# Duo attention and a one-slot-per-token expert layer on one core: loads, constants and steps put in another order

## The chip, the cores and the metric

The kernel runs on one core of a Trainium2 chip. Its engines are TensorE (PE, with its weight loads as PEld), VectorE (DVE), ScalarE (ACT), GpSimd (POOL) and SyncE (SP); sixteen DMA engines move data for the core. The metric is the device time of one execution in microseconds (us). TensorE's clock has two levels, 1.2 and 2.4 GHz, and the profile gives the granted clock as a share of the upper one.

## The reference

Attention first: 4 batches, 8 heads, 768 positions, 64 channels a head. Heads 0, 2 and 6 see all earlier positions; the other five see the first 4 positions and the last 64. The result, as a matrix of 3072 tokens by 512 columns, then goes through a layer of 8 experts in which a token uses at most one.

```python
scores = scale * np.matmul(q, k.transpose(0, 1, 3, 2))
stream_keep = causal & (is_sink | in_win)        # 4 sinks, window of 64
mask = np.where(retr[0, :, 0, 0, None, None], full_mask, stream_mask)
a = softmax(np.where(mask, scores, -1e9))
x = np.matmul(a, v)                               # -> [3072, 512]
...
do_compute = x @ w_skip > 0                       # the others keep x
e_idx = np.argmax(xc @ w_gate, axis=1)
gate_w = probs[np.arange(len(xc)), e_idx]
for e in range(8):                                # w1[e]: 512x1024, w2[e]: 1024x512
    h = np.maximum(xc[mask] @ w1[e], 0.0)
    y[mask] = gate_w[mask, None] * (h @ w2[e])
out[do_compute] = xc + y
```

## The kernel before

The program is written out by hand: instructions stand on each engine in the order in which the Python code makes them, and the framework adds the waits that data and buffers need. There is no scheduler, so a step that stands late in an engine's row, or that waits there, holds up all that stands behind it on that engine.

**Attention.** The loop at L554 goes over the four batches, b0 to b3. Each has six slots (`slots`, L524), and a slot is a few steps: `T(pr)` transposes q and k of a pair of heads (`trans`, L272: PE, then ACT copies qT and DVE copies kT), `R` makes the scores and exponentials of a full head (`retr`, L300: PE, then ACT), `X` those of a windowed head (`strm`, L322), `sinks` those of the four sink positions. The step `"o"` is `outs(g)` (L514): for row block g of the batch before, it multiplies the exponentials with v (`outp`, L359), normalises on DVE, stores the block to the output from SP's queue, and makes transposes (`xt`) and gate logits (`gates`) of earlier blocks. So v of a batch is used in the slots of the next one; `prep_v(b)` (L265), four DVE copies that shift v by half a block, is the first to wait for v of batch b.

**Loads.** All loads are issued from POOL's queue and cast fp32 to fp16 on the way: q and k of a batch (`load_qk`), v of a batch (`load_v`), the weights of an expert (`load_w`). There are two buffers for q and k, two for v, four for the weights of experts 0 to 3; the weights of experts 4 and 5 go into the buffers of q and k, those of 6 and 7 into memory that attention has left. `after_t` (L541), called in the slots, and the lines L572 to L575 between the batches issue them.

**Routing.** `route(c0, n)` (L412) makes, from the gate logits of n of the 24 row blocks, each token's expert and its place in a table; it is a generator, and `go_on` (L510) runs its next part. The first call takes blocks 0 to 11 in batch b3; after the last blocks of attention (the loop at L577, the tail) the second takes blocks 12 to 23.

**Experts.** With the table known, POOL gathers the rows of each expert, 2 tiles of 128 rows each (`gather`), and issues the last weights in between. Per expert PE makes the transposes (`xin`), the first product (`up_`) and the second (`down`), and POOL scatters the two tiles back to the output. The first scatter waits for every gather, since both touch the output tensor.

`fills` and the loops over `fp` are matmuls that no one reads.

## Time and profile before

| | |
|---|---|
| median of 3 runs | 260.56 us (260.16 to 263.18) |
| the profiled execution's own time | 263.12 us |
| its span in the profile | 261.3 us |
| PE busy | 189.6 us, 73% of the span |
| DVE busy | 115.3 us, 44% |
| ACT busy | 89.4 us, 34% |
| bytes read from memory | 56.66 MB |

No engine is busy throughout, and the share of an engine over the whole span mixes stages: the time is read stage by stage, by what ends the idle time in each. A busy time of POOL at a load is its issue; the data land later, which shows in the waits for them and in the rate of the DMA engines. The profiled execution took 2.56 us more than the median.

### The profile page before, as it was taken

To read this page: it belongs to the slowest core of one execution; us is meant where nothing else is said; L and a number is where in the kernel's file an instruction comes from. 1 tells how busy PE (TensorE), PEld (TensorE's weight loads), DVE (VectorE), ACT (ScalarE), POOL (GpSimd) and SP (SyncE) were. 2 spreads that over 40 slices of the span, in tenths; PEclk is the share of its full clock that TensorE was granted. 3 is DMA by queue.
4 is the path that set the end of the run, shared out by engine and by line. 5 is a ranking of instruction groups with operands and counts; after the bars stand their busy time and mean duration, and the time that the engine had idled before them with its cause. 6 is when DMAs were issued, how large, how long until landed. Compare 5 with 4: busy or idle time off the path is not lost.

```text
span 261.3 us, 5338 instructions
## 1 busy us (share of the span) xinstructions
PE 189.6 (73%) x2288; PEld 123.2 (47%) x2288; DVE 115.3 (44%) x280; ACT 89.4 (34%) x125; POOL 72.8 (28%) x84
## 2 busy tenths in 40 slices
PE   6302697769988706975939667997669999959960
PEld 2201354456765405654626344452456677726620
DVE  0008168467774025676693322471054454415430
ACT  3100575666683401582333432100232322313100
POOL 8605850031332000311000000006883400762260
PEclk9855599999995665897577955699799999999996
DMA  5999999999999999999970221103799993240110
GB/s 77 173 159 191 68 176 206 205 230 239 238 232 236 198 186 224 227 235 194 225 169 16 108 83 40 43 0 88 205 195 233 208 225 138 85 177 4 48 58 12
DMA packets 53138, 39.55 MB, mean 151 GB/s; under 512 B 27945, under 2 KB 44329, under 8 KB 53104
## 3 DMA queue, kind: packets, MB, share of 16 engines
q0 software_dynamic: 49648, 32.82, 84.7%
q1 hardware_dynamic: 3456, 6.29, 7.0%
q8 instruction: 20, 0.33, 0.5%
q14 instruction: 14, 0.11, 0.1%
HBM read 56.66 MB, written 10.49 MB: 257 GB/s over the span
## 4 chain that ended last, share of the span: by engine, by line
PE 53%; DMA 16%; DVE 12%; ACT 8%; issue 5%; POOL 3%; POOLq 0%; DVEq 0%; ACTq 0%
DMA va<-in_v_dram 15%; PE mhp L662 11%; PE myp L679 11%; PE sps L263 6%; ACT atr L319 5%; DVE x L384 3%; PE sps L315 3%; PE tps L277 3%; PE tps L398 3%; PE sps L329 2%; PE sps L311 2%; PE av L371 2%; ACT x L390 1%; PE mtp L646 1%; DMA xg<-out_dram,idg 1%
## 5 line engine op out<-in xcount | busy, mean ns | idle before, releaser
L319 ACT ACTIVATE atr<-sps 128x1024 f16<-128x1024 f32 (+1 forms) x36 | 31.5, 915 | 38.7 <-PE sps L315 38.7
L617 POOL DMA_INDIRECT xg<-out_dram,idg x16 | 16.5, 1029 | 68.4 <-DVE gs L608 59.2
L263 PE MATMUL sps<-esk,ident 128*128 128x512 f16 x90 | 27.7, 448 | 4.9 <-ACT atr L319 2.7
L398 PE MATMUL tps<-ident,x 128*128 128x128 f16 x96 | 11.5, 256 | 20.7 <-DVE x L392 10.9
L662 PE MATMUL mhp<-mxT,w1t 128*128 128x256 f16 x192 | 22.8, 278 | 4.0 <-issue 3.3
L683 POOL DMA_INDIRECT out_dram<-xg,idx x16 | 16.3, 1018 | 31.4 <-issue 17.3
L346 ACT ACTIVATE ats<-sps 128x768 f16<-128x768 f32 x20 | 15.4, 810 | 26.7 <-PE sps L340 26.7
L311 PE MATMUL sps<-tri,idl 64*128 64x128 f16 x144 | 12.4, 238 | 14.8 <-DVE tri L147 10.4
L662 PEld LDWEIGHTS <-w1t 128*128 128x128 f16 x192 | 19.3, 100 | 8.2 <-issue 5.0
L679 PE MATMUL myp<-w2t,ht 128*128 128x512 f16 x96 | 22.2, 379 | 0.0
L108 POOL DMA_DIRECT2D va<-in_v_dram x8 | 11.4, 1438 | 38.5 <-PE av L379 38.5
L283 DVE COPY kT<-tps 128x768 f16<-128x768 f16 x16 | 15.1, 947 | 15.5 <-PE tps L277 15.5
L681 DVE SCALAR_TENSOR_TENSOR xg<-myp,gs,xg 128x512 f32<-128x512 f32 x16 | 12.0, 751 | 22.1 <-PE myp L679 14.8
L398 PEld LDWEIGHTS <-x 128*128 128x128 f16 x96 | 6.8, 111 | 28.0 <-DVE x L392 11.4
L666 DVE TENSOR_SCALAR ht<-mhp 128x512 f16<-128x512 f32 x16 | 11.1, 691 | 17.1 <-PE mhp L662 15.0
L315 PE MATMUL sps<-qT,kT 64*128 64x512 f16 (+3 forms) x96 | 16.4, 352 | 3.0 <-DVE kT L283 3.0
L679 PEld LDWEIGHTS <-ht 128*128 128x128 f16 x128 | 12.3, 98 | 12.2
L668 ACT ACTIVATE ht<-mhp 128x512 f16<-128x512 f32 x16 | 9.6, 598 | 24.2 <-issue 12.9
L311 PEld LDWEIGHTS <-idl 64*128 64x128 f16 x144 | 8.0, 102 | 18.1 <-DVE idl L146 10.4
L283 ACT COPY qT<-tps 128x768 f16<-128x768 f16 x16 | 12.8, 800 | 10.3 <-PE tps L277 10.1
L263 PEld LDWEIGHTS <-ident 128*128 128x128 f16 x90 | 8.6, 107 | 15.5 <-issue 8.9
L651 ACT COPY mxT<-mtp 128x512 f16<-128x512 f16 x15 | 8.2, 588 | 19.2 <-PE mtp L646 13.1
(156 smaller groups left out, 342.7 us busy)
## 6 DMA issues: line engine op xcount, KB each, us to landing
w1t<-in_moe_w_dram POOLq DMA_DIRECT2D x6, 1024.0 KB
w2t<-in_moe_w_dram POOLq DMA_DIRECT2D x6, 1024.0 KB
out_dram<-x SPq DMA_DIRECT2D x24, 256.0 KB, 5.7
va<-in_v_dram POOLq DMA_DIRECT2D x8, 384.0 KB
qin<-in_q_dram POOLq DMA_DIRECT2D x3, 768.0 KB
kin<-in_k_dram POOLq DMA_DIRECT2D x3, 768.0 KB
qin<-in_moe_w_dram POOLq DMA_DIRECT2D x2, 1024.0 KB
kin<-in_moe_w_dram POOLq DMA_DIRECT2D x2, 1024.0 KB
```

Of the source, the lines that this page charges most:

```text
L263: nc.tensor.matmul(ps[:, :512], ident, fill, start=True, stop=True)
L283: eng(t.rearrange("c (p n) -> c p n", n=NT), ps.rearrange("c n p -> c p n"))
L311: nc.tensor.matmul(ps[i][:, x:x + P], idl[rows[i], u], tri[rows[i], u], start=(u == 0), stop=False, skip_group_check=True)
L315: nc.tensor.matmul(ps[i][:, x:x + n], kT[b, pr][rows[i], j * P:(j + 1) * P], qT[b, pr][rows[i], q0:q0 + n], start=False, stop=True, skip_g ...
L319: nc.scalar.activation(at[b, PAIRS[pr][i]][:, o:o + w], ps[i][:, :w], ACT.Exp, scale=SCALE)
L346: nc.scalar.activation(a, ps[i][:, :S], ACT.Exp, scale=SCALE)
L398: nc.tensor.matmul(ps[:, s], xs[g][:, s * P:(s + 1) * P], ident, is_transpose=True, start=(s == 0), stop=(s == DS - 1))
L617: nc.gpsimd.indirect_dma_start(out=xg[e, t], out_offset=None, in_=out[:, :], in_offset=bass.IndirectOffsetOnAxis(ap=idg[:, sl:sl + 1], axi ...
L662: nc.tensor.matmul(hp[:, u], w1t[:, s, f * P:(f + 1) * P], xT[:, s], start=(s == 0 and u == 0), stop=(s == DS - 1 and u == 1))
L679: nc.tensor.matmul(yp, hts[e][:, f, t * P:(t + 1) * P], w2t[:, f], start=(f == 0), stop=(f == FS - 1))
L681: nc.vector.scalar_tensor_tensor(xg[e, t], yp, gs[:, sl:sl + 1], xg[e, t], ALU.mult, ALU.add)
L683: sc = nc.gpsimd.indirect_dma_start(out=out[:, :], out_offset=bass.IndirectOffsetOnAxis(ap=idx[:, sl:sl + 1], axis=0), in_=xg[e, t], in_of ...
```

## The change

Seven edits stand in the diff. (1) The memsets of the ones column of both v buffers stand ahead of the first loads, and `vsk`'s memset stands in `consts_1`. (2) `load_qk(1)` goes ahead of `load_v(0)`. (3) Weights: `load_w(0)` moves from `consts_2` to `after_t(0)`, experts 1 to 4 to a new function `after_o` at the end of a batch, behind the load of v, and expert 5 into the expert stage, behind the first four gathers. (4) The slots hold their steps in another order, `prep_v` one slot later, `sinks` one slot earlier, and `go_on` is called once in a slot instead of twice. (5) Routing is done in three calls of 12, 6 and 6 blocks. (6) In the tail, `outp` of a block stands ahead of `xt` and `gates` of earlier ones; in the expert stage `cast(1)` stands ahead of `up_(0)`, and `xin(1)` in its middle. (7) Pools: the buffers of exponentials and v are in two pools by parity of the batch, qT has three buffers instead of four, and the expert tiles are taken from attention's space with waits tile by tile.

```diff
--- before.py
+++ after.py
@@ -81,13 +81,17 @@
     qkp = ctx.enter_context(tc.tile_pool(name="qkp", bufs=2))
     att = ExitStack()
-    ac = att.enter_context(tc.tile_pool(name="ac", bufs=1))
+    qtp = att.enter_context(tc.tile_pool(name="qtp", bufs=3))
+    par = [att.enter_context(tc.tile_pool(name=f"par{i}", bufs=1)) for i in range(2)]
+    xp = att.enter_context(tc.tile_pool(name="xp", bufs=3))
     q_in, k_in = {}, {}
-    va = [ac.tile([P, H, NT, V1], FP16, name=f"va{i}") for i in range(2)]
-    vs = [ac.tile([P, 5, NT, V1], FP16, name=f"vs{i}") for i in range(2)]
+    va = [par[i].tile([P, H, NT, V1], FP16, name=f"va{i}") for i in range(2)]
+    vs = [par[i].tile([P, 5, NT, V1], FP16, name=f"vs{i}") for i in range(2)]
     wts = {}
     def load_qk(b, split=False):
@@ -117,9 +121,11 @@
     rel_i = const.tile([P, P], I32, name="rel_i")
     nc.gpsimd.iota(rel_i, pattern=[[1, P]], base=0, channel_multiplier=-1)
+    for i in range(2):
+        nc.vector.memset(va[i][:, :, :, D:], 1.0)
     load_qk(0, True)
+    load_qk(1)
     load_v(0)
-    load_qk(1)
     esk = [const.tile([P, S], FP16, name=f"esk{i}") for i in range(2)]
@@ -131,8 +137,6 @@
     nc.vector.memset(ones, 1.0)
     warm = const.tile([P, 1], FP32, name="warm")
     nc.scalar.activation(warm, ones[:, :1], ACT.Exp)
-    for i in range(2):
-        nc.vector.memset(va[i][:, :, :, D:], 1.0)
     relh = const.tile([P, P], FP16, name="relh")
@@ -193,6 +197,7 @@
             nc.vector.memset(half[i * D:(i + 1) * D, i], 1.0)
         for t_ in skq:
             nc.vector.memset(t_, 0.0)
+        nc.vector.memset(vsk, 0.0)
     def consts_2():
         for i, h in enumerate(SINKS):
@@ -208,7 +213,6 @@
         nc.gpsimd.dma_start(out=WgAll[:, :, E],
                             in_=moe_w_skip.rearrange("(s p) -> p s", p=P))
         load_v(1)
-        load_w(0)
     def consts_3():
         nc.vector.memset(esk[1][:, :P], 0.0)
@@ -216,7 +220,6 @@
             nc.vector.memset(vs[i][D:, :, 0], 0.0)
     def consts_4():
-        nc.vector.memset(vsk, 0.0)
         nc.vector.tensor_scalar(bmask[:, :, 1], bm_i, 3.0, None, ALU.is_le)
         nc.vector.scalar_tensor_tensor(bmask[:, :, 1], bm_i, 0.0, bmask[:, :, 1],
@@ -235,10 +238,6 @@
         nc.vector.tensor_copy(vals[:, :, 0], tok_i)
-    qtp = att.enter_context(tc.tile_pool(name="qtp", bufs=3))
-    atr = att.enter_context(tc.tile_pool(name="atr", bufs=6))
-    ats = att.enter_context(tc.tile_pool(name="ats", bufs=10))
-    xp = att.enter_context(tc.tile_pool(name="xp", bufs=3))
     sp = att.enter_context(tc.tile_pool(name="sp", bufs=2, space=PSUM))
     tp = att.enter_context(tc.tile_pool(name="tp", bufs=2, space=PSUM))
     ap_ = att.enter_context(tc.tile_pool(name="ap", bufs=1, space=PSUM))
@@ -277,7 +276,7 @@
                     nc.tensor.matmul(ps[rows[i], n], src[b][:, h, n * D:(n + 1) * D], ident,
                                      is_transpose=True, start=(n == 0),
                                      stop=(n == NT - 1))
-            t = qtp.tile([P, S], FP16, tag=name, name=name, bufs=4 if dst is qT else 3)
+            t = qtp.tile([P, S], FP16, tag=name, name=name)
             dst[b, pr] = t
             eng = nc.scalar.copy if name == "qT" else nc.vector.tensor_copy
             eng(t.rearrange("c (p n) -> c p n", n=NT), ps.rearrange("c n p -> c p n"))
@@ -303,8 +302,9 @@
         ps = {}
         for i in ii:
             ps[i] = sp.tile([P, 1024], FP32, tag="s", name="sps")
-            if c == 0:
-                at[b, PAIRS[pr][i]] = atr.tile([P, RW], FP16, tag="atr", name="atr")
+            if (b, PAIRS[pr][i]) not in at:
+                at[b, PAIRS[pr][i]] = par[b % 2].tile([P, RW], FP16, tag="atr", name="atr",
+                                                           bufs=len(RETR))
         for x in (0, st):
             for u in range(2):
                 for i in ii:
@@ -341,7 +341,7 @@
                                      qt[rows[i], x:y], start=False, stop=True,
                                      skip_group_check=True)
         for i in ii:
-            a = ats.tile([P, S], FP16, tag="ats", name="ats")
+            a = par[b % 2].tile([P, S], FP16, tag="ats", name="ats", bufs=len(SINKS))
             at[b, PAIRS[pr][i]] = a
             nc.scalar.activation(a, ps[i][:, :S], ACT.Exp, scale=SCALE)
@@ -486,7 +486,7 @@
                                     lo16[:, hs].unsqueeze(2).to_broadcast([P, NT, P]),
                                     op=ALU.is_equal)
             yield
-            if h0:
+            if h0 + NT == n:
                 for i in range(n):
                     nc.tensor.matmul(tb, ol[:, i], mv[:, i], start=(i == 0),
                                      stop=(i == n - 1))
@@ -530,21 +530,28 @@
         both = (0, 1)
         return (
             (T(1), R(0, both, 0), "o"),
-            (T(2), R(0, both, 1), "o"),
-            (R(0, both, 2), T(3), lambda: after_t(b), "o", X(1, (0,))),
-            (R(1, (1,), 0), R(1, (1,), 1), lambda: prep_v(b), "o"),
-            (X(2, both), "o", R(1, (1,), 2)),
-            (T(0, b + 1) if b + 1 < B else (lambda: None), X(3, both), "o",
-             lambda: sinks(b)),
+            (R(0, both, 1), "o", X(1, (0,))),
+            (T(2), R(0, both, 2), "o", R(1, (1,), 2)),
+            (R(1, (1,), 0), R(1, (1,), 1), "o", T(3), lambda: after_t(b)),
+            (X(2, both), lambda: prep_v(b), "o", lambda: sinks(b)),
+            (T(0, b + 1) if b + 1 < B else (lambda: None), X(3, both), "o"),
         )
     def after_t(b):
         if b + 2 < B:
             load_qk(b + 2)
-            load_w(b + 1)
-        else:
-            load_w(b + 2, qkp, ("qin", "kin"))
+        if b == 0:
+            load_w(0)
+    def after_o(b):
+        if 1 <= b < 3:
+            load_v(b + 1)
+            load_w(b)
+        if b == 2:
+            load_w(3)
+            load_w(4, qkp, ("qin", "kin"))
     fills(10)
     consts_1()
@@ -561,34 +568,39 @@
                     f()
             if b == 0:
                 fills(3)
-            if g >= HALF + 2 and not routing:
+            if g == HALF + 2:
                 routing = route(0, HALF)
-            go_on()
             go_on()
             if b == 0 and i == 0:
                 consts_2()
             if b == 0 and 2 <= i < 5:
                 (consts_3, consts_4, consts_5)[i - 2]()
-        if 1 <= b < 3:
-            load_v(b + 1)
-        if b == 1:
-            load_w(3)
+        after_o(b)
+    g0 = (B - 1) * NT
     for i in range(NT + 2):
-        outs((B - 1) * NT + i, True)
+        if i < NT:
+            outp(g0 + i, True)
+        if i < NT + 1:
+            xt(g0 + i - 1, True)
+        gates(g0 + i - 2)
         fills(2)
         go_on()
+        if i == 1:
+            for _ in routing:
+                pass
+            routing = route(HALF, NT)
     for _ in routing:
         pass
     fills(6)
-    for _ in route(HALF, HALF):
+    for _ in route(HALF + NT, NT):
         fills(6)
     att.close()
-    with tc.tile_pool(name="mx", bufs=1) as mxp, \
-         tc.tile_pool(name="wp2", bufs=E - NW - 2) as wp2, \
-         tc.tile_pool(name="m16", bufs=2) as m16, \
+    with tc.tile_pool(name="wp2", bufs=E - NW - 2, reuse_waits="tile") as wp2, \
+         tc.tile_pool(name="mx", bufs=1, reuse_waits="tile") as mxp, \
+         tc.tile_pool(name="m16", bufs=2, reuse_waits="tile") as m16, \
          tc.tile_pool(name="mt_ps", bufs=2, space=PSUM) as mtp, \
          tc.tile_pool(name="mh_ps", bufs=4, space=PSUM) as mhp, \
          tc.tile_pool(name="my_ps", bufs=2, space=PSUM) as myp:
@@ -619,7 +631,10 @@
                     in_offset=bass.IndirectOffsetOnAxis(ap=idg[:, sl:sl + 1], axis=0),
                     bounds_check=N - 1, oob_is_err=False)
-        for e in range(4):
+        for e in range(2):
+            gather(e)
+        load_w(NW + 1, qkp, ("qin", "kin"))
+        for e in range(2, 4):
             gather(e)
         load_w(NW + 2, wp2)
         for e in range(4, 6):
@@ -651,10 +666,12 @@
                     nc.scalar.copy(xT[:, :, t * P:(t + 1) * P], ps)
             xts[e] = xT
-        def up_(e):
+        def up_(e, then=None):
             w1t, xT = wts[e][0], xts[e]
             ht = m16.tile([P, FS, T2 * P], FP16, tag="ht", name="ht")
             for f2 in range(FS // 2):
+                if f2 == 2 and then:
+                    then()
                 hp = mhp.tile([P, 2, T2 * P], FP32, tag="mh", name="mhp")
                 for u in range(2):
                     f = 2 * f2 + u
@@ -697,9 +714,8 @@
         xin(0)
         for _ in range(4):
             nc.tensor.matmul(fp, ident, fill, start=True, stop=True)
-        up_(0)
         cast(1)
-        xin(1)
+        up_(0, lambda: xin(1))
         cnt = rt.tile([P, E], FP32, name="cnt")
         nc.vector.tensor_copy(cnt, cp)
         cmx = rt.tile([P, 1], FP32, name="cmx")
```

POOL, from the loads of v of batch 1 to the last load of attention (va is a buffer of v, qin and kin those of q and k, w1t and w2t the weights of an expert). Before:

```order
L108 DMA va_76<-in_v_dram 128x24x64 x2
L114 DMA w1t<-in_moe_w_dram 128x4x1024
L115 DMA w2t<-in_moe_w_dram 128x8x512
L102 DMA qin<-in_q_dram 128x8x384
L103 DMA kin<-in_k_dram 128x8x384
L114 DMA w1t<-in_moe_w_dram 128x4x1024
L115 DMA w2t<-in_moe_w_dram 128x8x512
L102 DMA qin<-in_q_dram 128x8x384
L103 DMA kin<-in_k_dram 128x8x384
L114 DMA w1t<-in_moe_w_dram 128x4x1024
L115 DMA w2t<-in_moe_w_dram 128x8x512
L108 DMA va_75<-in_v_dram 128x24x64 x2
```

The same engine and the same stretch in the changed kernel:

```order
L112 DMA va_85<-in_v_dram 128x24x64 x2
L106 DMA qin<-in_q_dram 128x8x384
L107 DMA kin<-in_k_dram 128x8x384
L118 DMA w1t<-in_moe_w_dram 128x4x1024
L119 DMA w2t<-in_moe_w_dram 128x8x512
L106 DMA qin<-in_q_dram 128x8x384
L107 DMA kin<-in_k_dram 128x8x384
L112 DMA va_84<-in_v_dram 128x24x64 x2
```

Ahead of v of batch 2 stood the weights of three experts and q and k of batches 2 and 3; now one expert's weights and q and k of the two batches stand there.

DVE, the first rows of the program (esk, ident, ones, relh are constants). Before:

```order
L127 MEMSET esk_95 128x384
L129 TENSOR_SCALAR ident<-rel_i 128x128
L131 MEMSET ones 128x128
L135 MEMSET va_75 128x48
L135 MEMSET va_76 128x48
L139 TENSOR_SCALAR relh<-rel_i 64x128
```

And in the changed kernel:

```order
L125 MEMSET va_84 128x48
L125 MEMSET va_85 128x48
L133 MEMSET esk_106 128x384
L135 TENSOR_SCALAR ident<-rel_i 128x128
L137 MEMSET ones 128x128
L143 TENSOR_SCALAR relh<-rel_i 64x128
```

The two memsets of the v buffers moved from behind the issue of the load into va_75 to the head of DVE's row, ahead of that issue.

POOL in the expert stage (xg_0 and xg_1 are the two tiles of an expert's gathered rows). Before:

```order
L617 DMA xg_0_2738<-out_dram,idg 128x512
L617 DMA xg_1_2742<-out_dram,idg 128x512
L617 DMA xg_0_2746<-out_dram,idg 128x512
L617 DMA xg_1_2750<-out_dram,idg 128x512
L617 DMA xg_0_2754<-out_dram,idg 128x512
L617 DMA xg_1_2758<-out_dram,idg 128x512
L114 DMA w1t<-in_moe_w_dram 128x4x1024
L115 DMA w2t<-in_moe_w_dram 128x8x512
```

And in the changed kernel:

```order
L629 DMA xg_0_2767<-out_dram,idg 128x512
L629 DMA xg_1_2771<-out_dram,idg 128x512
L118 DMA qin<-in_moe_w_dram 128x4x1024
L119 DMA kin<-in_moe_w_dram 128x8x512
L629 DMA xg_0_2779<-out_dram,idg 128x512
L629 DMA xg_1_2783<-out_dram,idg 128x512
L629 DMA xg_0_2787<-out_dram,idg 128x512
L629 DMA xg_1_2791<-out_dram,idg 128x512
L118 DMA w1t<-in_moe_w_dram 128x4x1024
L119 DMA w2t<-in_moe_w_dram 128x8x512
```

The weights of expert 5, into the buffers qin and kin, now stand behind the gathers of experts 0 and 1, ahead of those of experts 2 to 7.

## Rows read from the trace of the kernel before

**Rows 1.** Stages: length; busy PE, PEld, DVE, ACT, POOL; clock; DMA share; GB/s

```profile
0.00:25.10 25.10, 7.59 (x72) 3.68 (x73) 4.90 (x26) 3.08 (x4) 12.24 (x20) 0.72 1.48 151
25.10:48.60 23.50, 18.02 (x225) 9.77 (x227) 12.03 (x26) 14.55 (x18) 10.28 (x15) 0.86 1.43 156
48.60:70.50 21.90, 18.83 (x410) 13.89 (x410) 15.21 (x33) 14.51 (x18) 4.03 (x5) 1.00 1.22 228
70.50:109.10 38.60, 26.31 (x422) 18.84 (x420) 16.39 (x36) 15.34 (x19) 6.08 (x7) 0.69 1.44 220
109.10:142.60 33.50, 24.65 (x422) 17.75 (x420) 23.14 (x63) 14.82 (x19) 3.85 (x4) 0.75 1.10 173
142.60:165.30 22.70, 16.16 (x210) 10.26 (x211) 5.86 (x14) 8.51 (x14) 0.00 (x0) 0.69 0.22 82
165.30:177.80 12.50, 12.44 (x75) 5.64 (x73) 8.60 (x34) 0.28 (x1) 0.00 (x0) 0.88 0.00 1
177.80:261.30 83.50, 65.63 (x466) 43.37 (x464) 29.16 (x52) 18.28 (x32) 36.31 (x36) 0.95 0.55 131
```

**Rows 2.** Waits of engines, longest sums: total, times, longest

```profile
DVE relh L139 <- DMA va<-in_v_dram: 18.9, 1, 18.9
DVE vs L269 <- DMA va<-in_v_dram: 16.1, 2, 13.6
```

**Rows 3.** The chain that ended last, in order of time: start, length, what

```profile
71.26 25.20 DMA va<-in_v_dram
231.54 3.25 issue
```

**Rows 4.** POOL's timeline, two pairs of loads of v: start, length

```profile
5.95 2.89 POOL L108 DMA_DIRECT2D va<-in_v_dram  x2
69.86 2.82 POOL L108 DMA_DIRECT2D va<-in_v_dram  x2 [10.05 <-PE av L379]
```

**Rows 5.** PE's timeline at the start: the last transpose before the first scores

```profile
10.54 0.53 PE L277 MATMUL tps<-ident,kin 128*64 128x128 f16 x12 [0.89 <-ACT qT L283]
```

**Rows 6.** Stretches chosen for what the DMA engines moved: columns as in Rows 1

```profile
30.50:35.50 5.00, 3.84 (x57) 1.99 (x53) 1.26 (x3) 3.28 (x5) 2.07 (x3) 0.88 2.72 151
40.00:55.00 15.00, 10.96 (x214) 7.10 (x213) 10.51 (x24) 10.60 (x13) 0.00 (x0) 1.00 1.27 206
97.00:115.00 18.00, 14.69 (x265) 10.94 (x266) 12.03 (x28) 8.42 (x11) 2.81 (x2) 0.73 1.17 227
```

**Rows 7.** DMA issues: what, queue, how often, KB each

```profile
w1t<-in_moe_w_dram POOLq DMA_DIRECT2D x6, 1024.0 KB
out_dram<-x SPq DMA_DIRECT2D x24, 256.0 KB, 5.7
va<-in_v_dram POOLq DMA_DIRECT2D x8, 384.0 KB
qin<-in_q_dram POOLq DMA_DIRECT2D x3, 768.0 KB
```

**Rows 8.** PE's timeline in the tail: a transpose and what it waited for

```profile
145.84 0.40 PE L398 MATMUL tps<-ident,x 128*128 128x128 f16 x4 [1.15 <-ACT x L390]
```

**Rows 9.** DVE's timeline in the last routing: one of two like it

```profile
173.75 0.95 DVE L485 TENSOR_TENSOR ol<-iota,lo 128x768 f16<-128x768 f16 x1
```

**Rows 10.** Expert stage, timelines: first gathered tile, second product, first and last scatter

```profile
181.42 0.43 DVE L639 CAST mx<-xg 128x512 f16<-128x512 f32 x1 [4.14 <-DMA xg<-out_dram,idg]
194.41 3.65 PE L662 MATMUL mhp<-mxT,w1t 128*128 128x256 f16 x32 [0.78 <-ACT mxT L651]
222.63 1.04 POOL L683 DMA_INDIRECT out_dram<-xg,idx  x1 [15.49 <-issue]
253.81 0.98 POOL L683 DMA_INDIRECT out_dram<-xg,idx  x1 [0.74 <-DVE xg L681]
```

**Rows 11.** The same steps, T(3) to X(2), in b1 and in b2: columns as in Rows 1

```profile
55.60:64.00 8.40, 6.96 (x147) 5.06 (x144) 5.92 (x14) 4.74 (x7) 3.39 (x4) 1.00 1.16 239
77.50:89.90 12.40, 11.13 (x148) 7.59 (x144) 2.87 (x6) 4.85 (x6) 1.65 (x2) 0.59 1.33 227
```

## The prediction

> **What bounds the kernel now.** I read the stages first [rows 1], then the waits [rows 2], then the chain [rows 3], and only then single timelines. The eight stages are the start (0 to 25.1 us, up to the first scores), the batches b0 to b3, the tail, the last routing and the experts. The reader should compare b1, b2 and b3: PE has nearly the same count of instructions (410 and 422), yet they take 21.9, 38.6 and 33.5 us. b1 is attention with its data in place: PE 18.8 of 21.9 us at clock 1.00. The other two are attention that waits, and the clock falls with it (0.69 and 0.75).
>
> The waits name what is late. DVE stands 18.9 us at the start on the load of v, in front of constants that the first scores need, because a memset into the v buffer stands behind that load. It stands 13.6 us in b2 (of 16.1 in two waits) at `prep_v`, on v again [rows 2]. The chain agrees: its longest piece by far is the load of v for batch 2, 25.2 us from 71.26 [rows 3], which POOL issues at 69.86 [rows 4] behind everything older in its queue. So up to b2 the kernel is bound by the order of its loads, after that by PE with DVE and ACT in its way, and in the experts by PE (65.6 of 83.5 us).
>
> **What the DMA engines can do.** Three stretches give rates: 151 GB/s where v moves, 206 where q, k and weights move, 227 when stores run too [rows 6]. That v was served alone there, with an expert's weights already issued behind it, is why I take loads of this queue to be served in the order of issue. By size [rows 7] q and k of a batch are 1.57 MB, v 0.79, an expert 2.10, a stored block 0.26.
>
> **The change, part by part.** The base is the profiled execution, 263.12 us with a span of 261.3; I keep the 1.82 between them.
>
> Start. PE has the transposes for the first scores done at 11.1 us [rows 5]; scores start at 25.1 because DVE came late. With the memsets ahead of the load, DVE has its 4.90 us of work in this stage [rows 1] and `vsk`'s memset, moved forward: 2080 columns, by the 768 columns in 0.95 us of [rows 9] some 2.6. That is done near 8.4 us, before PE. Half a microsecond for the bias matmuls gives first scores at 11.6: **13.5 saved**. Bounds: 12.5 to 13.9.
>
> b0. `load_qk(1)` now goes ahead of v. Both and batch 0 are 3.15 MB at 206 and 0.79 at 151, 20.5 us, plus some 4 to get going: v lands near 25. `prep_v` and the multiply into `vsk` behind the small sink loads stand in the fourth and fifth of six slots, 11.6 + 4/6 of 23.5 = 27. So I take 23.5 as before, and 4 us more as the upper bound, since the small loads come behind v. b1 stays at 21.9.
>
> b2. `load_v` for batch 2 leaves at 11.6 + 23.5 + 21.9 = 57.0, when the buffer is free. By then the queue holds q and k of four batches, v of two, one expert, and beside it six stores: 10.0 MB at 227 and 1.6 at 151, with 6 us of starting and gaps, 60.5. v lands near 67; `prep_v`, one slot later than now, is due at 57.0 + 4/6 of 21.9 = 71.6. The wait goes, with 4 us to spare. Late next is PE itself. I take 23.0, near b1: **15.6 saved** (bounds 21.9 and, if the spare is lost twice over, 28). v of batch 3 has one expert ahead of it and is easier.
>
> b3. DVE has 23.1 us here against 15.2 in b1; the 7.9 more are the first routing, in two parts per slot. One part per slot sends about 2.2 of it into the tail (a pair of large steps, 0.95 [rows 9] and some 0.5, and the copies after it). Added in full to b1 the rest gives 27.6, hidden in full 21.9; with DVE then 20.9 us busy of some 22, I take 27.0, nearer to the first: **6.5 saved**. A shorter wait on v (2.5 us is the other part of the 16.1) is in it.
>
> Tail. Now each of six blocks has PE waiting 1.15 us for ACT's copy of the block just made [rows 8], 6.9 in all. With `outp` ahead of `xt` PE makes the next block meanwhile. But DVE gets the second routing (8.6 us for twelve blocks [rows 1], some 6.5 for six) and the 2.2 from b3 on top of its 5.9: 14.6 us, which with 3 or so at the end bounds the stage from below at 17.5. I take 19.5 of 22.7: **3.2 saved**; bounds 17 and 24, the latter if the routing steps land between a block and its normalisation.
>
> Last routing. Six blocks instead of twelve: one of two pairs of large DVE steps goes (0.95 [rows 9] and some 0.5), and the DVE work of 8.6 shrinks towards 6.5; the waits of PE and DVE on each other stay. 9.5 instead of 12.5: **3.0 saved**, bounds 8.5 and 11. The first gather is then issued at 136.0 instead of 177.8.
>
> Are the weights there by then? Up to that point 23.1 MB at 227, v's 3.15 at 151 and 6 us make 128.7. So expert 4's weights land some 7 us before the first gather. Costed at nothing, under that cover.
>
> Experts. Moving `xin(1)` into `up_(0)` removes the wait of 0.78 ahead of the second product [rows 10]. Against it, expert 5's weights now stand in front of twelve gathered tiles. Between the first gather (177.8) and the first scatter, which waits for the last gathered tile (222.63), 16 tiles and two experts' weights went through: 8.4 MB in 44.8 less 3.6 (first gather to first tile at 181.42), or 204 GB/s, 10.3 us an expert, 1.3 a tile. So the first scatter moves from +44.8 to +55.1 after the first gather; sixteen at 1.3 put the last at +74.6, while now it is at +76.0, behind the last product. Hidden by 1.4 us. The gathers themselves: an expert takes (253.81 - 194.41)/8 = 7.4 us, expert 2's transposes are due near +22 and its tiles land at 3.6 + 5 x 1.3 + 10.3 = 20.4; expert 6 is due at 51.6 and ready, with its cast, at 52.2. Late by 0.6 to 2, I take 1.8. With the 0.78: **1.0 lost**. Bounds: 3 gained, if the stop of 3.25 us at 231.54 [rows 3], of which I know no cause, doesn't return, and 8 lost, if the late gathers add up. The tile-by-tile waits on attention's memory save nothing here, since gathers wait for the table and the stores anyhow.
>
> Sum: -13.5 - 15.6 - 6.5 - 3.2 - 3.0 + 1.0 = -40.8, so 222.3 for an execution like the profiled one. That one was 2.6 above the median; against the median I forecast **220 us**.
>
> **A rule that speaks against the first edit.** The two issues of v took 2.89 us with DVE standing still (5.95 us) and 2.82 with DVE at work (69.86) [rows 4]. The Trainium skill, SBUF — State Buffer, section "SBUF: two separate sides", says that a DMA issued from GpSimd waits while DVE runs certain copies, since its descriptors can't be written then. By it the constants, now running while the first loads are issued, would hold those loads back. The rows bear none of it out, and it makes a rival below.
>
> **The rivals.**
> - *Loads still late.* If stores and small loads take more of the DMA engines than 6 us, `prep_v` waits in b0, b2 and b3, four to five us each, and the last gather queues behind expert 4: 13 us, 233. For it: only 4 and 7 us to spare. Against: b1, with all of this going on, had none.
> - *Experts bound by the queue.* The first gathers meet expert 4's weights and expert 5's delay shows in full: one expert's 10.3 us, 230. For it: the stage's DMA share is high only while weights move, and now three move there. Against: the 7 us to spare.
> - *The order isn't what decides.* If the engines share between all loads outstanding, v of batch 2 stays late: the 15.6 of b2 come back, 235. Against: the stretch at 151 GB/s [rows 6].
> - *DVE holds back POOL at the start.* Then the first loads lose up to DVE's 7.5 us, 227.
> - *Slower: the clock.* The same steps took 8.4 us at clock 1.00 and 12.4 at 0.59 [rows 11], 1.48 times. The clock fell in the stages in which PE stood [rows 1]. Should the new order leave short stands everywhere, so that all 124 us of attention after the start ran so, they would take 60 us more: 279. It eats the gain once about two thirds of attention runs at the lower level (1.2 GHz); now it is under half. Against: the long stands go.
>
> **How the numbers follow.** Chances: forecast 0.66, loads late 0.14, experts 0.10, order 0.04, POOL 0.03, clock 0.03. The forecast's own bounds, taken together, reach some 9 down (b2 1, b3 4, tail 2, routing 1, experts 4, not all at once) and 10 up; loads late, experts and order lie within 18. The range is 210 to 238. A measurement of this kernel tells about 2% (5 us) from no change. All cases but the last are faster by more than that; of its 0.03 I give 0.01 to within 2% and 0.02 to slower.
>
> **What would show it.** In the changed kernel: first scores near 11.6 us and no wait of DVE at its constants; no wait of DVE on va over 2 us in b2 or b3, b1 to b3 all between 21 and 28 us; the tail's transposes without a wait for ACT; the first gather near 136; the first scatter some 55 us after it, the last some 76. Wrong would be: any of these loads landing after its step, a low clock through b1 to b3, or PE in the experts standing for gathered tiles more than 2 us at a time.

## The result, and the profile after

The changed kernel takes 224.83 us (median of 4 runs, 223.65 to 226.33) beside 260.36 us of the kernel before: a ratio of 0.8619, 95% interval 0.8551 to 0.8687. The profiled execution took 224.89 us, its span is 223.1. That is 38.2 us less span than before, where the sum said 40.8. (Of the kernels below, the profiled executions of numbers 1, 2, 3, 7 and 11 ran over 1.5% longer than the fastest run of the same kernel, so their stages are read with that margin.)

The page first: PE and the clock over the span, in 40 slices.

```profile
PE   6858666999889696987786996687799999938920
PEclk9999995599999969999799799589999999996995
```

The stages of the changed kernel, with the same borders as [rows 1] (columns as there: start, b0, b1, b2, b3, tail, last routing, experts):

```profile
0.00:10.62 10.62, 7.74 (x70) 3.47 (x72) 7.34 (x27) 3.08 (x4) 9.65 (x16) 1.00 0.81 113
10.62:31.73 21.11, 15.45 (x229) 8.73 (x223) 7.49 (x19) 14.65 (x18) 8.82 (x14) 1.00 1.61 141
31.73:57.72 25.99, 22.22 (x409) 16.05 (x410) 17.46 (x38) 15.03 (x19) 4.65 (x6) 0.80 1.47 213
57.72:82.00 24.28, 20.80 (x430) 15.30 (x426) 16.61 (x35) 15.62 (x20) 4.46 (x4) 0.93 1.46 224
82.00:104.16 22.16, 18.90 (x419) 14.09 (x413) 19.21 (x53) 14.51 (x19) 7.80 (x8) 1.00 1.45 221
104.16:124.38 20.22, 14.86 (x240) 10.31 (x237) 15.73 (x52) 7.54 (x15) 0.00 (x0) 0.87 1.14 248
124.38:134.60 10.22, 10.16 (x57) 4.57 (x55) 6.54 (x33) 0.24 (x1) 0.00 (x0) 0.92 0.76 141
134.60:223.10 88.50, 67.75 (x465) 44.28 (x463) 29.47 (x52) 18.37 (x32) 37.87 (x38) 0.91 0.63 148
```

Beside before and the forecast, in us:

| stage | before | forecast | after |
|---|---|---|---|
| start | 25.1 | 11.6 | 10.6 |
| b0 | 23.5 | 23.5 | 21.1 |
| b1 | 21.9 | 21.9 | 26.0 |
| b2 | 38.6 | 23.0 | 24.3 |
| b3 | 33.5 | 27.0 | 22.2 |
| tail | 22.7 | 19.5 | 20.2 |
| last routing | 12.5 | 9.5 | 10.2 |
| first gather at | 177.8 | 136.0 | 134.6 |
| experts | 83.5 | 84.5 | 88.5 |

The gain is where it was looked for, and two stages got longer: b1 by 4.1 and the experts by 5.0. The timelines say why. First the end of b0 and the start of b1, DVE and PE:

```profile
28.64 2.52 DVE L230 TENSOR_TENSOR vsk<-vraw,bmask 20x520 f16<-20x520 f16 x4 [4.25 <-DMA vraw<-in_v_dram]
34.85 0.85 PE L276 MATMUL tps<-ident,kin 128*64 128x128 f16 x12 [2.60 <-DVE kT L282]
```

DVE stands 4.25 us for the sink rows (`vraw`), whose small loads wait behind v. Its copies of kT come late, PE stands 2.60 us for one, and then runs from 33.8 to 44.0 at the lower clock:

```profile
33.80:44.00 10.20, 8.35 (x100) 5.55 (x101) 5.20 (x12) 4.18 (x5) 0.83 (x1) 0.50 1.68 199
```

In b2 the wait for v that answers to [rows 2] is still there, with 1.86 us instead of 13.6:

```profile
75.44 0.56 DVE L268 COPY vs<-va 64x1560 f16<-64x1560 f16 x1 [1.86 <-DMA va<-in_v_dram]
```

In the experts, PE stands twice for the tiles of expert 2, and once for 4.09 us at 201.40; the rows that answer to [rows 10] are the first and the last scatter, 51.3 and 79.9 us behind the first gather:

```profile
156.78 0.40 PE L661 MATMUL mtp<-ident,mx 128*128 128x128 f16 x4 [1.84 <-DVE mx L654]
158.22 0.40 PE L661 MATMUL mtp<-ident,mx 128*128 128x128 f16 x4 [1.04 <-DVE mx L654]
201.40 5.14 PE L679 MATMUL mhp<-mxT,w1t 128*128 128x256 f16 x32 [4.09 <-ACT mxT L666]
...
185.90 1.05 POOL L700 DMA_INDIRECT out_dram<-xg,idx  x1 [12.88 <-DVE ht L683]
214.51 0.98 POOL L700 DMA_INDIRECT out_dram<-xg,idx  x1 [0.74 <-DVE xg L698]
```

### The profile page after: what moved, and what is told of

It reads as the page before. It is cut to its first block, busy times and chain, and to the rows that moved or that the text cites. A ratio compares the mean times of both kernels' runs of the same rounds, so it can differ in the third digit from the quotient of the medians.

```text
span 223.1 us, 5346 instructions
## 1 busy us (share of the span) xinstructions
PE 177.9 (80%) x2283; PEld 116.8 (52%) x2283; DVE 119.9 (54%) x304; ACT 89.0 (40%) x126; POOL 73.3 (33%) x84
## 5 line engine op out<-in xcount | busy, mean ns | idle before, releaser
L262 PE MATMUL sps<-esk,ident 128*128 128x512 f16 x84 | 25.1, 435 | 4.6 <-DVE ident L135 1.8
L679 PE MATMUL mhp<-mxT,w1t 128*128 128x256 f16 x192 | 25.0, 295 | 4.1 <-ACT mxT L666 4.1
L679 PEld LDWEIGHTS <-w1t 128*128 128x128 f16 x192 | 20.2, 106 | 9.3 <-issue 4.9
L696 PE MATMUL myp<-w2t,ht 128*128 128x512 f16 x96 | 22.2, 379 | 0.0
L683 DVE TENSOR_SCALAR ht<-mhp 128x512 f16<-128x512 f32 x16 | 10.9, 689 | 20.8 <-PE mhp L679 10.5
L685 ACT ACTIVATE ht<-mhp 128x512 f16<-128x512 f32 x16 | 9.6, 597 | 28.6 <-issue 13.4
L698 DVE SCALAR_TENSOR_TENSOR xg<-myp,gs,xg 128x512 f32<-128x512 f32 x16 | 11.9, 750 | 14.4 <-PE myp L696 13.6
L282 ACT COPY qT<-tps 128x768 f16<-128x768 f16 x16 | 12.8, 798 | 11.5 <-PE tps L276 11.5
L398 PE MATMUL tps<-ident,x 128*128 128x128 f16 x96 | 10.2, 232 | 7.9 <-DVE x L392 4.1
L262 PEld LDWEIGHTS <-ident 128*128 128x128 f16 x84 | 7.8, 106 | 13.2 <-issue 6.9
L315 PE MATMUL sps<-qT,kT 64*128 64x512 f16 (+3 forms) x96 | 14.2, 325 | 0.0
L654 DVE CAST mx<-xg 128x512 f16<-128x512 f32 x15 | 6.4, 448 | 12.7 <-DMA xg<-out_dram,idg 12.6
L311 PE MATMUL sps<-tri,idl 64*128 64x128 f16 x144 | 10.8, 226 | 2.7 <-ACT atr L319 2.0
L384 DVE TENSOR_TENSOR x<-av,rec 128x512 f32<-128x512 f32 x18 | 12.5, 692 | 0.6
```

The source lines that it names most:

```text
L262: nc.tensor.matmul(ps[:, :512], ident, fill, start=True, stop=True)
L282: eng(t.rearrange("c (p n) -> c p n", n=NT), ps.rearrange("c n p -> c p n"))
L315: nc.tensor.matmul(ps[i][:, x:x + n], kT[b, pr][rows[i], j * P:(j + 1) * P], qT[b, pr][rows[i], q0:q0 + n], start=False, stop=True, skip_g ...
L384: nc.vector.tensor_tensor(x.rearrange("p c t d -> p t c d"), avo[:, :, :, :D], rec.unsqueeze(3).to_broadcast([P, 2, 4, D]), op=ALU.mult)
L679: nc.tensor.matmul(hp[:, u], w1t[:, s, f * P:(f + 1) * P], xT[:, s], start=(s == 0 and u == 0), stop=(s == DS - 1 and u == 1))
L696: nc.tensor.matmul(yp, hts[e][:, f, t * P:(t + 1) * P], w2t[:, f], start=(f == 0), stop=(f == FS - 1))
```

## Experiments

Twelve kernels in three sets; the runs of a set share a chip and the runs of the kernel before (median 257.71, 261.57 and 258.06 us). So ratios to the kernel before are compared across sets, and microseconds only within one.

**1. The start alone, on the kernel before.**

```
+    for i in range(2):
+        nc.vector.memset(va[i][:, :, :, D:], 1.0)
     load_qk(0, True)
     load_v(0)
```
(and the same two lines gone from behind the loads)

> The kernel before with one edit: the two memsets into the v buffers stand ahead of the first loads. My theory (the terms of the sum are separate): first scores near 11.6 us instead of 25.1, and the whole 13.5 us arrives at the end, since POOL also issues its later loads that much earlier: 247 us, with the wait of prep_v for v of batch 2 still there, at 13 us or so. Rival (the loads' queue absorbs it): the queue moves bytes at the same pace, v of batch 2 still lands near 96 us, the wait of prep_v grows from 13.6 to some 25 us, and the end stays at 258 to 260 us.

Ratio 0.998 (0.982 to 1.015), 258.22 us: nothing. First scores came at 10.44 us, and all of it was given back. Two pieces of the chain of this kernel (start, length):

```profile
33.18 26.47 DMA kin<-in_k_dram
66.24 30.25 DMA va<-in_v_dram
```

And its b1 and b2 (columns as in the stages):

```profile
32.79:65.47 32.68, 21.21 (x409) 15.26 (x408) 15.28 (x33) 14.62 (x18) 7.22 (x9) 0.84 1.35 217
65.47:109.73 44.26, 22.80 (x423) 16.83 (x421) 16.39 (x36) 15.21 (x19) 6.10 (x7) 0.73 1.43 215
```

k of batch 2, issued at 33.18, lands at 59.7 behind v of batch 1 and the weights of expert 0, and v of batch 2 lands at 66.24 + 30.25 = 96.5, to the tenth where it landed before, 71.26 + 25.20 [rows 3]. The queue of loads is the pace; whoever arrives earlier waits longer (prep_v 19.3 us in b2 instead of 13.6). My theory of a term of its own fell, the rival holds.

The same run answers the rule that I weighed. Here DVE works through its constants (0.98 to 6.12 us) while POOL issues the six loads of q and k of batch 0; in the kernel before DVE stood still from 1.48 us on. The six took 0.75 to 0.91 us each in both. POOL's pair for v took as long as in [rows 4], 2.89 us, but DVE worked for only 1.1 us beside it:

```profile
5.96 2.89 POOL L108 DMA_DIRECT2D va<-in_v_dram  x2
```

The Trainium skill, SBUF — State Buffer, section "SBUF: two separate sides", has a DMA issued from GpSimd wait while DVE runs certain copies; the trace shows no such wait beside these memsets, fp16 copies and TENSOR_SCALARs, and says nothing of others. What did get longer are five of DVE's own steps: 0.34 to 0.52 us, where they took 0.17 to 0.28 in the kernel before. Why isn't shown.

**2. The order of the loads alone, on the kernel before.**

```
-        load_w(0)                      # behind load_v(1)
...
+        if b == 0:
+            load_w(0)
...
-            load_w(b + 1)
...
             load_v(b + 1)
+            load_w(b)
```
(and experts 3 and 4 behind that of batch 2; expert 5 stays)

> The kernel before with the weights of experts 0 to 4 behind q, k and v as in the changed kernel, and nothing else (the memsets still behind the load of v, the old slots, expert 5 at its old place). My theory (loads served in the order of issue): the wait of prep_v for v of batch 2 goes from 13.6 us to under 2, b2 takes 23 to 25 us instead of 38.6, b3 loses its 2.5 us wait on v: 242 to 245 us. Rival (the engines share between all loads that are outstanding): v of batch 2 is late as before, 258 to 261 us.

Ratio 0.942 (0.930 to 0.954), 243.01 us: 14.7 us. The wait for v in b2 is gone altogether, b2 takes 25.65 us instead of 38.6, and the forecast of 242 to 245 held. The rival (shared engines, v as late as before) is out.

```profile
70.19:95.84 25.65, 23.44 (x422) 17.00 (x421) 16.40 (x36) 15.22 (x19) 4.29 (x5) 0.80 1.19 177
```

**3. The start undone, on the changed kernel.** The two memsets go back behind `load_v(0)`.

> The changed kernel with the two memsets into the v buffers back behind the load of v, and nothing else. In the kernel before this edit alone was worth nothing, since the queue of loads set the pace up to 96 us. Theory A (with the new order of the loads the queue is no longer the pace, so the start counts in full): v lands at 24 us, first scores near 30 instead of 10.6, the first gather 14 to 19 us later, 238 to 243 us where the changed kernel takes 224. Theory B (the start is absorbed here as well): later waits shrink by what the start loses, within 3 us of the changed kernel.

Ratio 0.924 (0.906 to 0.943), 239.29 us, against 0.862 with the edit: about 16 us. Beside number 6 of the same set, which differs from the changed kernel only in the tail, it is 19.9 us by the medians. DVE stands for v, which now lies behind q and k of batch 1:

```profile
27.75 0.41 DVE L143 TENSOR_SCALAR relh<-rel_i 64x128 f16<-64x128 int32 x1 [26.27 <-DMA va<-in_v_dram]
```

First scores come at 34.63, 24.0 us late, the first gather at 156.85 instead of 134.6, 22.3 late where I expected 14 to 19. So theory A, and more of it: the same edit is worth nothing in front of a queue that sets the pace, and nearly its whole length at the first gather once the loads are in order. The start and the order of the loads are not two terms; the order is worth 15 alone, the start only with it.

**4. Two routing steps per slot, on the changed kernel.** One more `go_on()` in each slot of b3.

> The changed kernel with two routing steps per slot in b3 as before, and nothing else. My prediction's step (DVE's routing work in b3 is on the path, a part of it sent into the tail saves time): b3 takes 2 to 4 us more, the tail some 2 less, and the end comes 0 to 3 us later. Rival (b3 was long because of low clock and late loads, and the spreading of the routing is worth nothing): b3, tail and end all within 1 us of the changed kernel.

236.19 us beside 223.70 of the changed kernel in the same set: 12.5 slower (ratio 0.916, 0.899 to 0.932), four times the most that I expected. b3 (columns as in the stages):

```profile
80.81:116.29 35.48, 24.84 (x430) 17.81 (x425) 23.60 (x62) 15.32 (x20) 7.80 (x8) 0.81 1.35 223
```

Two of PE's stands in it, from its timeline:

```profile
94.24 0.20 PE L437 MATMUL rps<-oh,utri 128*128 128x96 f16 x1 [2.73 <-DVE oh L432]
112.17 0.50 PE L491 MATMUL tbp<-mv,ol 128*128 128x64 f16 x6 [4.25 <-DVE ol L485]
```

With two steps in a slot, PE's part of the routing stands right behind DVE's part in the program, so PE, which works in order, waits until DVE has got through what stands in its own queue. With one step a whole slot of attention lies between. b3 is 13.3 us longer than in the stages above: these two stands and a third of 0.93 are 7.9 us, and PE's longer busy time at the lower clock (24.84 us at 0.81 for 18.90 at 1.00) is 5.9. So PE's place behind DVE is on the path. That the amount of DVE's work (23.60 us for 19.21) isn't, is not shown: the edit moves both. The kernel before has the same waits:

```profile
122.81 0.26 PE L437 MATMUL rps<-oh,utri 128*128 128x96 f16 x1 [2.44 <-DVE oh L432]
134.18 0.50 PE L491 MATMUL tbp<-mv,ol 128*128 128x64 f16 x6 [1.71 <-DVE ol L485]
137.15 0.50 PE L491 MATMUL tbp<-mv,ol 128*128 128x64 f16 x6 [2.47 <-DVE ol L485]
```

**5. The old slots, on the changed kernel.** The table of slots as before, four buffers for qT.

> The changed kernel with the old table of slots (T(2) and T(3) one slot earlier, prep_v in the fourth slot instead of the fifth, sinks at the end of the sixth; four buffers for qT as before), and nothing else. Theory A (the table matters by its deadlines: prep_v stands one slot, some 3.7 us, earlier, so the wait for v of batch 2 grows from 1.9 us to 5 or 6 and the wait for the sink rows in b0 too): 4 to 8 us slower. Theory B (the table matters by the even load of PE between slots): every batch 1 to 2 us longer without a longer wait for v, 3 to 7 us slower. Theory C (it doesn't matter): within 2 us.

231.06 us beside 223.70: 7.4 slower. b3 takes 22.87 us, 1.4 more than in the changed kernel of this set (21.45), and b1 0.6 less, so the even spread of PE's work is worth little. b2 took 26.54 with the wait for v at 4.37:

```profile
75.86 0.56 DVE L268 COPY vs<-va 64x1560 f16<-64x1560 f16 x1 [4.37 <-DMA va<-in_v_dram]
```

That is theory A, with a wait a little shorter than forecast. In the changed kernel of this set b2 takes 21.7 us (59.52 to 81.26) without that wait, so b2 gives 4.8 of the 6.1 us that are there at the first gather (138.15 against 132.04). The two profiled executions differ by 9.3; the rest lies in the experts, where the stop of number 10 was longer here. prep_v's deadline makes most of what the table is worth.

**6. The old order inside a block of the tail, on the changed kernel.** `outs(g0 + i, True)` instead of `outp`, `xt`, `gates`.

> The changed kernel with the old order inside a block of the tail (transpose of the block before, its gates, then the next block), and nothing else. My prediction's step (PE stands 1.15 us a block for ACT's copy): each of six blocks waits over 1 us again, the tail takes 22.5 to 24 us instead of 20.2, 2 to 4 us slower. Rival (with the second routing in the tail DVE is the bound): the waits are there, but the tail is as long as before within 1 us.

Ratio 0.856 (0.837 to 0.875), no slower. The tail takes 20.79 us instead of 20.22, although PE's waits for ACT's copy are back (5.8 us in five, against 3.1 in two). The rival's number holds: the order inside a block is worth nothing beside the second routing. Its reason isn't shown, since DVE is busy for 13.63 us here and for 15.73 in the changed kernel:

```profile
104.57:125.36 20.79, 14.90 (x234) 10.05 (x231) 13.63 (x45) 7.97 (x14) 0.00 (x0) 0.84 1.15 241
```

**7. The last routing over twelve blocks, on the changed kernel.** The second half is not split.

> The changed kernel with the last routing over twelve blocks at once, as before, and nothing else. My prediction's step: the last routing takes 12 to 13 us instead of 9.2 to 10.2. In the tail DVE is freed of some 6.5 us of work. If DVE bounds the tail, it gets 1.5 to 3 us shorter and the net is 0 to 1.5 us slower; if not, the tail stays at 20.2 and the net is 2.5 to 3.5 us slower.

220.23 us beside 258.06 before, a ratio of the medians of 0.853. Tail and last routing of this kernel:

```profile
105.22:123.94 18.72, 14.91 (x226) 9.97 (x223) 10.47 (x26) 7.39 (x14) 0.00 (x0) 0.82 1.14 247
123.94:135.28 11.34, 11.28 (x75) 5.46 (x74) 8.59 (x34) 0.28 (x1) 0.00 (x0) 1.00 0.83 161
```

Together 30.06 us, in the changed kernel 20.22 + 10.22 = 30.44. What the split takes off the routing (1.1) it puts into the tail (1.5): worth nothing that can be told. DVE is freed of 5.3 us in the tail, and the tail gets 1.5 shorter, so DVE bounds it only in part.

**8. All gathers ahead of expert 5's weights, on the changed kernel.**

```
-        for e in range(2):
+        for e in range(E):
             gather(e)
         load_w(NW + 1, qkp, ("qin", "kin"))
-        for e in range(2, 4): ...
```

> The changed kernel with all sixteen gathers ahead of the weights of experts 5, 6 and 7. The last gather should land some 25 us after the first instead of some 50, and the first scatter follow it, so that no row of eleven scatters in a stretch builds up. Theory A (the late gathers and the stop of all engines near 194 to 201 us come from this queue): the waits of 1.8 and 1.0 us for the tiles of expert 2 go, the stop of some 4 us goes, and with it the stretch at clock 0.5 after it: 216 to 218 us. Theory B (the stop has nothing to do with the scatters): only the 2.9 us of the late tiles go, 222 us, with a stop of 3 to 5 us still in the experts. Theory C (the weights are late now): expert 5's weights are due 46 us after the first gather and land at 25 + 10 = 35, expert 7's are due at 61 and land at 56; if PE waits for them, 225 to 230 us.

Ratio 0.832 (0.823 to 0.840). The last gather is issued at 152.80, 19.8 us after the first (37.4 in the changed kernel), PE no longer stands for expert 2, and no weight is late. The experts take 78.69 us:

```profile
133.01:211.70 78.69, 65.80 (x465) 43.70 (x463) 29.66 (x52) 18.27 (x32) 37.17 (x38) 0.92 0.76 166
```

This looked like theory A, stop included. But the next kernel, in the same set, has no stop either.

**9. The sink rows early, on the changed kernel.** The five `vraw` loads stand between q and k of batches 0 and 1.

> The changed kernel with the five small loads of the sink rows of v (vraw) directly behind q and k of batch 0, ahead of q and k of batch 1 and of v. Theory A (the wait of 4.25 us of DVE for vraw at the end of b0, and the clock of 0.5 from 33.8 to 44.0 us behind it, are what b0 and b1 lost against my prediction): that wait is gone, b1's first scores come at some 31 to 32 us instead of 36.0, the low clock there shrinks or goes: 219 to 221 us. Theory B (something else is late next, v of batch 1 or the copies of DVE): 223 to 225 us.

Ratio 0.843 (0.834 to 0.851). The wait of 4.25 us went, and v came in its place, since its load now stands behind five more:

```profile
31.16 0.56 DVE L268 COPY vs<-va 64x1560 f16<-64x1560 f16 x1 [3.66 <-DMA va<-in_v_dram]
```

b1 starts at 32.20 (before this edit 31.73): theory B, in place. The better time has another source: its experts, gathers and twelve scatters in a row as in the changed kernel, took 81.73 us without a stop.

**10. The changed kernel again.**

> The changed kernel itself, beside the others. Its profiled execution had a stop of all engines of some 4 us near 194 to 201 us, in the experts, while eleven scatters went out in a row; the kernel with the sink loads early had twelve such scatters in a row and no stop. Theory A (the stop belongs to an execution or to a chip, not to the scatters or to the kernel): none here, experts of 82 to 84 us from the first gather to the end instead of 88.5, 218 to 221 us in all. Theory B (the stop belongs to this kernel): it is there again, 224 us, some 5 us above the two kernels that have none.

223.70 us, ratio 0.865, and a stop at the same place:

```profile
197.01 5.32 PE L679 MATMUL mhp<-mxT,w1t 128*128 128x256 f16 x32 [3.32 <-issue]
```

By the words of the expectation that is theory B. With all runs in view it is not the kernel: such a stop, in which PE, ACT and DVE lag behind each other and ACT or DVE stands for 3 us or more without a load being late, is in the experts of all four kernels of this set, of the changed kernel and of the kernel before ([rows 3], 231.54), and of none of the eight others, four of which have eleven or twelve scatters in a row as it has (numbers 3, 6, 7 and 9). What makes it stays open; a set is also a chip here, and the two can't be told apart.

**11. Gathers first and sink rows early.**

> The changed kernel with both edits of the two kernels before: all gathers ahead of the weights of experts 5 to 7, and the sink loads of v behind q and k of batch 0. Theory A (the two gains are separate, since one lies at the end of b0 and one in the experts): first gather at 132, experts 79 us, 211 to 213 us. Theory B (one hides the other or the queue binds): no better than the kernel with the gathers alone, 213 to 215 us.

218.73 us beside 223.70 in this set, ratio 0.844 (0.825 to 0.864). 2% below the changed kernel, whose interval (0.836 to 0.895) overlaps, and no better than the gathers alone. b1 gets short in it (22.37 us at clock 1.00), but then DVE waits 5.14 us for v in b2, and the first gather comes at 136.03 instead of 132:

```profile
75.41 0.56 DVE L268 COPY vs<-va 64x1560 f16<-64x1560 f16 x1 [5.14 <-DMA va<-in_v_dram]
```

Theory B, as far as the intervals tell.

**12. Gathers first, and v and the sink rows ahead of q and k of batch 1.**

```
     load_qk(0, True)
+    load_v(0)
+    for i, h in enumerate(SINKS): ...  # vraw
     load_qk(1)
-    load_v(0)
```

> The changed kernel with all gathers ahead of the weights of experts 5 to 7, and at the start the order q and k of batch 0, v, the sink rows, q and k of batch 1. With the sink rows ahead of q and k of batch 1 and v behind them, the wait of 4.25 us for the sink rows was replaced by one of 3.66 us for v. Theory A (v first takes that wait away as well): DVE waits neither for v nor for the sink rows over 1 us, b1's first scores at 32 us instead of 36, some 3 to 6 us faster than with the gathers alone, a ratio to the kernel before of 0.81 to 0.825. Theory B (q and k of batch 1 are late now): their transposes, due at 28 us, wait, and the ratio is as with the gathers alone, 0.83 to 0.845.

211.56 us, ratio 0.825 (0.815 to 0.836), below the changed kernel's whole interval (whose profiled executions held the stop). b1 takes 20.54 us at clock 1.00, where the changed kernel took 25.99 at 0.80, and DVE waits for no load in it:

```profile
31.65:52.19 20.54, 18.80 (x411) 14.07 (x411) 14.56 (x31) 15.03 (x19) 1.75 (x2) 1.00 1.33 225
```

So the chain wait, stand, low clock in b1 is shown by its removal. The others fit it roughly: for its first kT of b1 PE stood 2.88, 2.60, 1.90, 1.64 us and not at all (number 8, the changed kernel, 9, 11, 12), and b1 took 25.46, 25.99, 24.52, 22.37 and 20.54 us at clock 0.87, 0.80, 0.86, 1.00 and 1.00. Of some 5 us in b1, 2.4 arrive at the first gather (130.58 against 133.01 of the gathers alone); b2 gives the rest back (25.15 against 23.3). Why, seven kernels say together (the changed one and numbers 4, 5, 6, 8, 9 and 11): in all of them DVE gets v of batch 2 at 74.9 to 75.9 us, after a wait, though b2 starts anywhere from 54.4 to 59.0. Here it comes at 72.23:

```profile
72.23 0.56 DVE L268 COPY vs<-va 64x1560 f16<-64x1560 f16 x1 [1.46 <-DMA va<-in_v_dram]
```

In b2 the queue of loads still sets the pace, so what b1 gains turns into waiting there. Theory A in place and mechanism; in time it can't be told from the gathers alone, whose interval overlaps.

## Why the prediction was right, and where not

**Start.** Right, 10.6 for 11.6. But the working made it a term of its own, and it isn't one (experiments 1 and 3). It could be added only because b2's term was in the same sum.

**b0 and b1.** The upper bound in "b0", 4 us for small loads behind v, is what came: DVE's 4.25 us, with its price falling just across the border into b1. The value that I took, nothing, was wrong by that, and by the prediction's own sign (a load landing after its step) so was the step. The term that failed is "some 4 to get going": v was to land near 25 and landed at 27.9 (POOL's wait in the last section), the sink rows behind it at 28.6, for steps due at 27. The kernel before had shown the larger term:

```profile
7.36 12.78 DMA va<-in_v_dram
```

There v had landed at 20.1, behind q and k of batch 0. At the sum's own rates those 1.57 and 0.79 MB take 12.8 us, so getting going took 7.3; with 7.3 the sum gives 27.8. The sum also lacked the second price, 10.2 us at clock 0.50.

**b2.** Right, 24.3 for 23.0, and for the reason given: the queue serves in the order of issue (experiment 2). The spare of 4 us wasn't there: v landed at 75.4 instead of near 67, after 1.86 us of wait. Two sizes were wrong. The sum had six stores where ten were issued by then, 1.05 MB more, some 4.6 us at 227. And it had 151 GB/s for v where the engines moved 92 and then 28, since POOL had issued nothing large between v of batch 0 and v of batch 1 (last section):

```profile
22.00:28.00 6.00, 4.31 (x66) 2.37 (x64) 1.50 (x6) 4.18 (x6) 1.40 (x3) 1.00 2.37 92
28.00:31.00 3.00, 2.10 (x56) 1.50 (x56) 2.36 (x4) 1.67 (x3) 3.00 (x3) 1.00 0.43 28
```

**b3.** Right in direction, wrong in reason and size: 11.3 saved for 6.5. The step said that DVE's 7.9 us of extra work lengthen b3 and one step per slot moves 2.2 of it on. DVE was nearly as busy as forecast (19.21 us for 20.9) and b3 was short all the same, at clock 1.00. The three stands of PE on routing tiles in the kernel before (6.6 us) and the low clock with them (PE busy 24.65 us for 18.90) are gone: what counts is how far PE stands behind the DVE step that it needs (experiment 4). The prediction had DVE's busy time in that place.

**Tail and last routing.** 30.4 for 29.0. Neither edit is worth anything beside the other (experiments 6 and 7), where my sum gave each its own 3 us. That both want DVE is the likely reason, not a shown one; no kernel has both taken out. The waits for ACT that the new order was to remove sum to 6.0 us in the kernel before, not 6.9.

**Experts.** 5.0 lost for 1.0. The late tiles of expert 2 cost 2.9 us where I took 1.8; over the kernels with this order of gathers it is 0.9 to 4.9. The first scatter came at +51.3 for +55.1, the last at +79.9 for +74.6 (hidden behind the last product, as said). The rest is the stop, for which I had only the hope that it wouldn't return. Without it, 81.18 and 81.73 us (experiments 6 and 9) stand against 79.31 and 80.65 for the old stage (experiments 1 and 2): a loss of 0.5 to 2.4, around the forecast term.

**The rivals.** Loads late: in small, at b1 and b2, 5.4 us of its 13. Experts bound by the queue: no; moving the gathers up took away waits of 2.9 us, not 10. Engines sharing: out. DVE holding back POOL: out. Low clock: in b1 above all (0.80).

The errors nearly cancel, which is luck: b0, b3 and the start were better by 8.2, b1, b2, tail, routing and experts worse by 10.8 against the sum. Those 2.6 and the 2.3 that I took off for the median (the changed kernel's profiled execution lies at its median) are the 4.8 between 220 and 224.83.

## What to carry to other kernels

Before a gain at the head of a queue is added to a gain further back, ask which of them sets the pace when the other is gone: here one edit was worth 0 alone and 16 to 20 after the other. On an engine that works in order, put the consumer of another engine's result one whole slot behind it; giving that distance up cost 12.5 us here (the edit moved DVE's work too). Order loads by when they are needed, the very small ones too, and ask what a stand costs afterwards in clock.

## What the runs showed of the hardware

- POOL's DMAs waited here for the DMA issued eight places earlier. These four waits are, in order, for q and k of batch 1 and for the two loads of v:

```profile
17.91 0.57 POOL L204 DMA_DIRECT2D vraw<-in_v_dram  x1 [3.29 <-DMA qin<-in_q_dram]
...
21.78 0.80 POOL L211 DMA_DIRECT2D WgAll<-in_moe_w_gate_dram  x1 [2.63 <-DMA kin<-in_k_dram]
24.98 0.76 POOL L213 DMA_DIRECT2D WgAll<-in_moe_w_skip_dram  x1 [2.41 <-DMA va<-in_v_dram]
27.93 2.93 POOL L112 DMA_DIRECT2D va<-in_v_dram  x2 [2.20 <-DMA va<-in_v_dram]
```

So seven small loads hold back the large one behind them: v of batch 1 is issued at 27.93, though POOL had issued v of batch 0 by 10.5. It is also why the start alone didn't bring the loads of experiment 1 forward: v of batch 1 is issued at 27.88 there, and at 27.50 in the kernel before.
- The stop in the experts comes and goes with the set of runs, not with the kernel (6 of 14 profiled executions; PE's longest single wait in it was the 5.89 us of the kernel with the old slots, while in the kernel with two routing steps none was over 0.85).
